# A transformer block with recurrent memory, forward and backward: products over a three-head block of tokens write 120 instead of 128 columns

## The chip, the cores and the metric

The kernel runs on one core of one Trainium2 chip. The metric is device microseconds per execution. A core has a TensorE (matrix products out of SBUF into PSUM), VectorE, ScalarE and GpSimd (in the profile PE, DVE, ACT and POOL; PEld is TensorE's loading of weights), and SyncE (SP), which here issues transfers. A matmul takes a stationary operand, loaded beforehand ("weights", lhsT), and streams a moving operand (rhs) past it: `out = lhsT.T @ rhs`. A turn (transpose) is a matmul whose moving operand is the identity.

## What is computed

Two blocks with an adaptive layer norm: an attention that carries eight memory tokens from segment to segment, and a gated feed-forward. The outputs are the block's result and the gradients of eleven inputs. Cut to the part around the change:

```python
for s in range(n_seg):                                   # 64 segments of 32 tokens
    h = jnp.concatenate([mem, x[:, s*32:(s+1)*32]], axis=1)   # 8 + 32 = 40 tokens
    q = jnp.einsum('btd,dhe->bhte', h, Wq)               # 32 heads of 128
    k = jnp.einsum('btd,dhe->bhte', h, Wk)
    v = jnp.einsum('btd,dhe->bhte', h, Wv)
    scores = jnp.einsum('bhqe,bhke->bhqk', q, k) * scale
    scores = jnp.where(mask[None, None], scores, -1e9)
    p = _softmax(scores, axis=-1)
    o = jnp.einsum('bhqk,bhke->bhqe', p, v)
    o = jnp.einsum('bhte,hed->btd', o, Wo)
    mem = o[:, :8]                                       # carried on
    outs.append(o[:, 8:])
...
_out, _vjp = jax.vjp(_f, ...)                            # and the gradients
```

Since the memory is carried, the 64 segments run one after another, forward in one direction and backward in the other.

## The kernel before

After a short setup, four stages follow each other on the core: the forward recurrence (`phase2`, roughly 30 to 1010 us), the feed-forward with its backward (`phase3`, to about 1525 us), the backward recurrence (`phase4`, to about 2510 us) and the gradients of the attention's weights (`phase5`, to the end).

**Tiling of the recurrences.** Three heads of 40 tokens are put side by side: 120 tokens. 32 heads make `G` = 11 such groups. Each group has a slot of `GW` = 128 columns in tiles of 11 x 128, so eight columns of each slot belong to no token. The groups are worked in `NP` = 3 parts of at most `PG` = 4 groups (4, 4 and 3); a part fills one PSUM bank. `part3(t, pi)` is a view of a part's slots in an SBUF tile.

**A forward round** (one segment). PE projects q, k and v, turns them, forms the scores (L724, whose moving operand has 120 columns), ACT takes the exponentials into ET, PE forms O (L759), DVE and ACT scale it into `Ost` (token rows, 120 of 128 filled, the rest zero). `ott(pi)` turns `Ost` by `transposes_part` (L737): four matmuls with the identity (L742) per part, and `evac` (L56; its copies show as L61 on ACT, L63 on DVE) copies the result to OT. The output projection (L223, `at_ps`) reads OT; OT and Ost are stored for the backward.

**A backward round** (one segment; loop from NS-1 to 0 in `phase4`). The order of every engine's instructions is the order of the code, fixed by `pin`. On PE, in this order:

- the projection of dy through Wo's transpose (L255) into RAd; `turn` (L1480): turns of RAd, which ACT and DVE copy into dOT (slots of 120 columns)
- dV' first part (`grad_mm("dVT", dOst, Pst, 0)`, L1614): weights dOst, moving Pst
- `dp` (L1593): weights dOT, moving VT, three parts; meanwhile DVE forms dO x O in place in OT (`prod`, L1578)
- dV' second part; `dost(2)`: turns of dOT (L1526); then `ds` (L1601): weights OT, moving a tile of -1, added onto dP in the same PSUM bank; DVE makes dS of it, times scale and Pst (L1603)
- dVT times Wv's transpose (L215), dV' third part, dV rows (`grad_mm("dV", Pst, dOst)`, weights Pst, moving dOst)
- `dstt`: turns of dS (L1526), copied to dST by ACT, DVE, ACT
- dK' (weights Qst, moving dS), copied to dKT by DVE; dQ' (`grad_mm("dQT", Kst, dST)`, weights Kst, moving dST), copied to dQT by ACT
- dKT, the rest of dVT and dQT times the weights' transposes (L215, L223), sums over the heads (L323), ACT's copy into the next round's dyT, and the next projection

In ACT's order stand, around the turns of dS: dVT part 2, dV rows part 0, dST part 0, dV rows part 2, dST part 2, then the three parts of dQT. In DVE's: dV rows part 1, dST part 1, the three parts of dKT.

SP loads OT, PS and VT (352 KB each) a round ahead into two buffers, and Qst and Kst (120 rows of the 128) into one buffer each; it also issues the DMA transposes of the whole dKT and dQT into rows, which POOL stores. POOL copies RAd into rows 0 to 95 of dOst; the rows of the tails come by three small DMAs of POOL (`dO_tails`, L1546).

Ahead of the loop, `ptiles` (L1425) makes the tiles and clears those with `zero=True` by a POOL memset (L1430): dS, dOst, then Qst and Kst. dST, dVT, dKT and dQT are not cleared. Behind the memsets POOL copies the first round's tails into dOT (L65) and issues dOst's first DMAs; SP's first loads of Qst and Kst wait for these tiles' memsets.

Of the kernel before, what the change touches and what calls it, by code (L numbers as in the profile page):

```python
# [40 lines left out]
class K:  # L41
# [395 lines left out]
    def phase2(self):  # L437
        nc, tc, cfg, io = self.nc, self.tc, self.cfg, self.io
        D, DC, H, E, L, M, T, G, NS = cfg.D, cfg.DC, cfg.H, cfg.E, cfg.L, cfg.M, cfg.T, cfg.G, cfg.NS
        GW = 128  # L440
        NP = 3
        PG = 4
# [8 lines left out]
        with ExitStack() as ctx:  # L451
# [13 lines left out]
            def ps_b16(name):  # L465
                return psp.tile([128, PG, GW], BF16, name=name, tag="p")

            def ptiles(name, n, zero=True, w=G * GW):
                ts = []
                for i in range(n):  # L470
                    t = pt.tile([128, w], BF16, name=f"{name}{i}")
                    if zero:
                        zeros.append(lambda t=t, w=w: nc.vector.memset(t[:, 1024:w] if w == 9 * 128 else t[:], 0.0))
                    ts.append(t)
                return ts
# [7 lines left out]
            Ost = ptiles("Ost", 1)[0]  # L483
            OT = ptiles("OT", 1)[0]
# [71 lines left out]
            def part3(t, pi):  # L556
                return t[:, pi * PW:min((pi + 1) * PW, G * GW)].rearrange("p (g x) -> p g x", x=GW)
# [131 lines left out]
            for s in range(NS):  # L689
# [44 lines left out]
                    a, b = a * PG, min(b * PG, G)  # L734
                    nc.vector.reciprocal(rden[:, a:b], ps[0:120, PG - 1, a:b])

                def transposes_part(src, pi, w=GW):  # L737
                    ps = ps_b16("tps")
                    n = min(PG, G - pi * PG)
                    for j in range(n):  # L740
                        g = pi * PG + j
                        nc.tensor.transpose(ps[:, j, :], src[:, g * w:g * w + GW], self.ident[:, :])  # L742
                    return ps[:, 0:n, :], n

                def vshift():
                    sh = ps_f32("sh_ps")
# [25 lines left out]
                                            rden[:, pi * PG:pi * PG + n].unsqueeze(2).to_broadcast([120, n, 128]), op=ALU.mult)  # L772

                def ott(pi):
                    ps, n = transposes_part(Ost, pi)
                    self.evac("dve" if pi == 1 else "act", part3(OT, pi)[:, 0:n, :], ps)

                def outproj():
                    ps = psp.tile([128, 256], F32, name="at_ps", tag="p")
# [57 lines left out]
                Pst = sb2.tile([128, G, 128], BF16, name="Pst", bufs=1)  # L837
# [29 lines left out]
                if more and not turned:  # L867
                    mask_mm(more.pop(0))
                    mask_mm(more.pop(0))
                ott(0)  # L870
                if len(more) > 1:
                    mask_mm(more.pop(0))
                ott(1)
                if len(more) > 1:
                    mask_mm(more.pop(0))
                ott(2)
                if more:
                    mask_mm(more.pop(0))
# [39 lines left out]
            for pi in range(NP):  # L918
                ps, n = transposes_part(ET, pi)
# [4 lines left out]
            for pi in range(NP):  # L924
                ps, n = transposes_part(Vst, pi)
# [472 lines left out]
    def phase4(self):  # L1398
        nc, tc, cfg, io = self.nc, self.tc, self.cfg, self.io
        D, DC, H, E, L, M, T, G, NS = cfg.D, cfg.DC, cfg.H, cfg.E, cfg.L, cfg.M, cfg.T, cfg.G, cfg.NS  # L1400
        GW = 128
# [4 lines left out]
        with self.p4_ctx as ctx:  # L1406
            WqT, WkT, WvT, WoT, negones = self.WqT, self.WkT, self.WvT, self.WoT, self.negones
# [8 lines left out]
            PG = 4  # L1416
            PW = PG * GW

            def ps_f32(name):
                return psp.tile([128, PG, GW], F32, name=name, tag="p")  # L1420

            def ps_b16(name):
                return psp.tile([128, PG, GW], BF16, name=name, tag="p")

            def ptiles(name, n, zero=True):  # L1425
                ts = []
                for i in range(n):
                    t = pt.tile([128, G * GW], BF16, name=f"{name}{i}")
                    if zero:
                        nc.gpsimd.memset(t[:], 0.0)  # L1430
                    ts.append(t)
                return ts

            dOT = pt.tile([128, cfg.XW], BF16, name="dOT")
# [4 lines left out]
            dSs = ptiles("dS", 1)  # L1439
            dSTs = ptiles("dST", 1, zero=False)  # L1440
            dOst_t = ptiles("dOst", 1)[0]
            dXTs = {nm: ptiles(nm, n, zero=False) for nm, n in (("dVT", 1), ("dKT", 1), ("dQT", 1))}

            def part3(t, pi):
                return t[:, pi * PW:min((pi + 1) * PW, G * GW)].rearrange("p (g x) -> p g x", x=GW)
# [72 lines left out]
                    loads[s] = d  # L1518
                return loads[s]

            def transposes_part(src, pi, w=GW):
                ps = ps_b16("tps")
                n = min(PG, G - pi * PG)
                for j in range(n):
                    g = pi * PG + j
                    nc.tensor.transpose(ps[:, j, :], src[:, g * w:g * w + GW], self.ident[:, :])  # L1526
                return ps[:, 0:n, :]

            def load_rows(t, dram, s):
                if s >= 0:  # L1530
# [29 lines left out]
            for s in reversed(range(NS)):  # L1560
# [11 lines left out]
                VT, OT, Pst, Kst, Qst = ld["VT"], ld["OT"], ld["Pst"], Kst_t, Qst_t  # L1572
                dS, dST, dOst = dSs[0], dSTs[0], dOst_t
                dVT, dKT, dQT = dXTs["dVT"][0], dXTs["dKT"][0], dXTs["dQT"][0]
# [13 lines left out]
                def dp(pi):  # L1588
                    ps = dps[pi] = ps_f32("dp_ps")
                    n = min(PG, G - pi * PG)  # L1590
                    for j in range(n):
                        g = pi * PG + j
                        nc.tensor.matmul(ps[:, j, :], lhsT=dOT[:, g * 120:g * 120 + GW], rhs=VT[:, g * GW:(g + 1) * GW],  # L1593
                                         start=(j == 0), stop=False, skip_group_check=True)

                def ds(pi):
                    ps = dps[pi]
                    n = min(PG, G - pi * PG)
                    for j in range(n):
                        g = pi * PG + j  # L1600
                        nc.tensor.matmul(ps[:, j, :], lhsT=OT[:, g * GW:(g + 1) * GW], rhs=negones[:, :],  # L1601
                                         start=False, stop=True, skip_group_check=True)
                    nc.vector.scalar_tensor_tensor(out=part3(dS, pi), in0=ps[:, 0:n, :], scalar=cfg.scale, in1=part3(Pst, pi),  # L1603
                                                   op0=ALU.mult, op1=ALU.mult)

                def grad_part(nm, lh, rh, xt, pi, eng):
                    grad_out(nm, xt, pi, eng, grad_mm(nm, lh, rh, pi))

                def grad_mm(nm, lh, rh, pi):
                    ps = ps_f32("g_ps")  # L1610
                    n = min(PG, G - pi * PG)
                    for j in range(n):
                        g = pi * PG + j
                        nc.tensor.matmul(ps[:, j, :], lhsT=lh[:, g * GW:(g + 1) * GW], rhs=rh[:, g * GW:(g + 1) * GW],  # L1614
                                         start=True, stop=True)
                    return ps

                def grad_out(nm, xt, pi, eng, ps):
                    self.evac(eng, part3(xt, pi), ps[:, 0:min(PG, G - pi * PG), :])
                    if pi == NP - 1 and nm != "dVT":  # L1620
                        rows = rxp.tile([128, G, 128], BF16, name="rows_x")
                        nc.sync.dma_start(rows[:], xt[:, :], transpose=True)
                        dram = {"dKT": self.DKR, "dQT": self.DQR}[nm][s]
                        row_stores.append(lambda: nc.gpsimd.dma_start(dram, rows[:]))
# [5 lines left out]
                    self.evac(eng, rv_rows[:, pi * PG:pi * PG + n, :], ps[:, 0:n, :])  # L1630

                def dstt(pi):
                    ps = transposes_part(dS, pi)
                    self.evac("dve" if pi == 1 else "act", part3(dST, pi), ps)

                dh_ps = [None]
                n_dh = [0]
# [27 lines left out]
                turn(0)  # L1665
                turn(1)
                gv0 = grad_mm("dVT", dOst, Pst, 0)
                prod(0)
                dp(0)
                prod(1)  # L1670
                dp(1)
                prod(2)
                dp(2)
                gv1 = grad_mm("dVT", dOst, Pst, 1)
                grad_out("dVT", dVT, 0, "act", gv0)
                if b_done:
                    b_done()
                dost(2)
                grad_out("dVT", dVT, 1, "act", gv1)
                ds(0)  # L1680
                ds(1)
                ds(2)
                self.pop_later()
                dht(dVT, WvT, 0)
# [17 lines left out]
                rv_out(0, "act", gr0)  # L1702
                rv_out(1, "dve", gr1)
                dstt(0)
                rv_out(2, "act", gr2)
                row_stores.append(lambda s=s, rows=rv_rows: nc.gpsimd.dma_start(self.DVR[s], rows[:]))
                dstt(1)
                dstt(2)
                gks = [grad_mm("dKT", Qst, dS, pi) for pi in range(NP)]
                load_rows(Qst_t, self.QST, s - 1)  # L1710
# [22 lines left out]
                g = s // 4  # L1733
# [428 lines left out]
```

## Time and profile before

| | us |
|---|---|
| three runs | 3092.86, 3091.20, 3092.27 |
| median | 3092.27 |
| the profiled execution: span from its first to its last instruction | 3090.4 |

The mean granted TensorE clock over the span is 0.991 of full speed. A "busy" matmul is one that has been issued and has not ended; matmuls overlap, so busy time is not the time that a matmul costs. In the lines of the prediction a row of the timeline is: start us, how long the row lasts us, engine, line, operation, out<-in, partitions x columns, and xN, the number of instructions merged in the row; in brackets, the idle time of the engine before it and what ended it. For a matmul the shape reads rows * columns of the weights, then partitions x columns of the result. The longest groups of the backward recurrence on PE, for a sense of proportion (lines of the page; count, busy us, mean ns):

| line, what | count | busy us | mean ns |
|---|---|---|---|
| L215 dh_ps<-WvT,dVT, 512 columns | 2048 | 133.6 | 381 |
| L223 dhq_ps<-WqT,dQT, 256 columns | 4096 | 122.9 | 273 |
| L215 dh_ps<-WkT,dKT, 512 columns | 2048 | 122.3 | 380 |
| L1614 g_ps<-Pst_l,dOst, 128 columns | 704 | 71.8 | 221 |
| L1593 dp_ps<-VT_l,dOT, 128 columns | 704 | 60.8 | 222 |
| L1614 g_ps<-dST,Kst, 128 columns | 704 | 59.5 | 218 |

### The profile page before, as it was taken

The numbers are of one execution on the slowest core, as the hardware profiler recorded it, in microseconds if no ns is written. First come the engines' busy times: TensorE is split into PE (matmuls) and PEld (weight loads), VectorE is DVE, ScalarE is ACT, GpSimd is POOL, SyncE is SP. The second block draws the span as 40 slices with busy tenths as digits, with TensorE's granted clock in tenths as the row PEclk, the third lists the DMA queues.
The fourth block names the chain that finished last, engine by engine and source line by source line (L and its number), as shares of the span: only waits on it lengthen the run. The fifth ranks groups of instructions, "written<-read, shape, count | busy, mean of one in ns | idle before, by whom it ended". The sixth has DMA issues, their size and how long they took to land.

```text
span 3090.4 us, 106123 instructions
## 1 busy us (share of the span) xinstructions
PE 3001.3 (97%) x43845; PEld 1831.6 (59%) x43845; DVE 1630.0 (53%) x3799; ACT 1268.9 (41%) x3056; POOL 1379.6 (45%) x2958
## 2 busy tenths in 40 slices
PE   6999999999998899989999999999999999999999
PEld 3666666666665444445577777777777754445455
DVE  4556656665555788732255555555555642322221
ACT  2555555555555433322255555555555530111011
POOL 3666766667766222211244444444444422333322
PEclk8999999999999999999999999999999999999999
DMA  8888788788778899997599999999999998666574
GB/s 299 215 216 202 203 211 215 205 211 216 200 201 261 201 232 230 226 280 246 169 237 245 246 244 242 241 248 242 247 240 246 243 277 282 197 197 220 191 238 147
DMA packets 845992, 703.54 MB, mean 228 GB/s; under 512 B 544354, under 2 KB 717954, under 8 KB 845124
## 3 DMA queue, kind: packets, MB, share of 16 engines
q1 hardware_dynamic: 714196, 486.69, 62.4%
q0 software_dynamic: 60656, 148.64, 15.1%
q10 hardware_dynamic: 70656, 61.41, 6.3%
q8 instruction: 345, 5.65, 0.8%
q14 instruction: 139, 1.14, 0.1%
HBM read 294.93 MB, written 276.35 MB: 185 GB/s over the span
## 4 chain that ended last, share of the span: by engine, by line
PE 86%; DMA 5%; issue 4%; DVE 2%; POOL 1%; SPq 1%; ACT 0%; POOLq 0%; DVEq 0%; ACTq 0%
PE pass_ps L255 18%; PE gps L1952 9%; PE dh_ps L215 8%; PE g_ps L1614 6%; PE gps5o L1966 4%; PE at_ps L223 4%; PE dhq_ps L223 4%; PE gps L1301 3%; PE mm L1145 3%; PE dh_tps L215 3%; PE turn_ps L264 2%; PE dp_ps L1593 2%; PE tps L1526 2%; PE tps L742 2%; PE mm L1105 2%
## 5 line engine op out<-in xcount | busy, mean ns | idle before, releaser
L1952 PE MATMUL gps<-rows,hrows 128*128 128x512 bf16 (+2 forms) x2160 | 417.5, 356 | 0.0
L1952 PEld LDWEIGHTS <-hrows 128*128 128x128 bf16 x2160 | 211.3, 98 | 204.5
L255 PEld LDWEIGHTS <-hT 128*32 128x32 bf16 x6144 | 158.6, 97 | 169.2 <-DMA Wq<-in_A_Wq_dram 6.0
L1658 POOL COPY dOst<-RAd 96x512 bf16<-96x512 bf16 x128 | 75.4, 612 | 312.7 <-DVE RAd L63 312.5
L63 DVE CAST ot<-gps 128x512 bf16<-128x512 f32 (+3 forms) x76 | 48.1, 634 | 288.3 <-PE gps L1952 198.4
L1956 POOL DMA_DIRECT2D out_dram<-ot x108 | 81.4, 753 | 255.4 <-DVE ot L63 140.2
L61 ACT ACTIVATE ot<-gps 128x512 bf16<-128x512 f32 (+3 forms) x75 | 41.3, 551 | 355.1 <-PE gps L1952 216.1
L909 POOL TENSOR_TENSOR Pst<-Pst,rden 120x1408 bf16<-120x1408 bf16 x63 | 159.7, 2534 | 49.4 <-issue 21.8
L61 ACT ACTIVATE dVT<-g_ps 128x512 bf16<-128x512 f32 (+1 forms) x192 | 109.5, 570 | 96.3 <-PE g_ps L1614 95.6
L63 DVE CAST RA0v<-pass_ps 128x512 bf16<-128x512 f32 x128 | 88.6, 692 | 90.4 <-PE pass_ps L255 86.8
L255 PE MATMUL pass_ps<-Wv,hT 128*32 128x512 bf16 x2048 | 134.2, 382 | 0.0
L215 PE MATMUL dh_ps<-WvT,dVT 128*32 128x512 bf16 x2048 | 133.6, 381 | 0.2 <-DVE RBd L63 0.2
L1966 PE MATMUL gps5o<-WoT,rows 128*128 128x512 bf16 x592 | 128.5, 379 | 1.4 <-DMA rows<-OSR 1.4
L255 PE MATMUL pass_ps<-Wq,hT 128*32 128x512 bf16 x2048 | 123.3, 383 | 5.8 <-DMA Wq<-in_A_Wq_dram 5.8
L223 PE MATMUL at_ps<-Wo,OT 128*32 128x256 bf16 x4096 | 124.9, 275 | 3.8 <-DMA Wo<-in_A_Wo_dram 3.6
L255 PE MATMUL pass_ps<-Wk,hT 128*32 128x512 bf16 x2048 | 121.8, 380 | 2.2 <-ACT hT L899 1.1
L1603 DVE SCALAR_TENSOR_TENSOR dS<-dp_ps,Pst_l 128x512 bf16<-128x512 f32 (+1 forms) x192 | 112.1, 640 | 22.1 <-PE dp_ps L1601 22.1
L255 PE MATMUL pass_ps<-WoT,dyT 128*32 128x256 bf16 (+1 forms) x3072 | 122.5, 308 | 0.9 <-ACT dyT L1732 0.9
L223 PE MATMUL dhq_ps<-WqT,dQT 128*32 128x256 bf16 x4096 | 122.9, 273 | 0.0
L215 PE MATMUL dh_ps<-WkT,dKT 128*32 128x512 bf16 x2048 | 122.3, 380 | 0.0
L223 PEld LDWEIGHTS <-dQT 128*32 128x32 bf16 x4096 | 109.6, 97 | 15.8
L223 PEld LDWEIGHTS <-OT 128*32 128x32 bf16 x4096 | 103.9, 97 | 19.7 <-ACT OT L61 8.4
(419 smaller groups left out, 7073.6 us busy)
## 6 DMA issues: line engine op xcount, KB each, us to landing
OSR<-Ost SPq DMA_DIRECT2D x64, 352.0 KB
OT<-OT SPq DMA_DIRECT2D x64, 352.0 KB
VT<-VTr SPq DMA_DIRECT2D x64, 352.0 KB
PS<-Pst SPq DMA_DIRECT2D x64, 352.0 KB
OT_l<-OT SPq DMA_DIRECT2D x64, 352.0 KB
Pst_l<-PS SPq DMA_DIRECT2D x64, 352.0 KB
VT_l<-VT SPq DMA_DIRECT2D x64, 352.0 KB
DVR<-rows_x POOLq DMA_DIRECT2D x64, 352.0 KB, 6.2
```

The costliest lines, as they stand in the source:

```text
L61: return nc.scalar.activation(out, in_, AF.Copy)
L63: return nc.vector.tensor_copy(out, in_)
L215: self.nc.tensor.matmul(ps[32 * j:32 * j + 32, :], lhsT=lhsT, rhs=w, start=(n < 4), stop=(n >= total - 4), tile_position=(0, 32 * j))
L223: nc.tensor.matmul(ps[32 * j:32 * j + 32, :], lhsT=x[k], rhs=w[k][:, 256 * d:256 * d + 256], start=(n == 0), stop=(n == total - 1), tile_p ...
L255: self.nc.tensor.matmul(ps[32 * j:32 * j + 32, :], lhsT=lhs(c), rhs=rhs, start=(c == 0), stop=(c == DC - 1), tile_position=(0, 32 * j))
L909: nc.gpsimd.tensor_tensor(Pst[0:120, :, :], Pst[0:120, :, :], rden[:, :].unsqueeze(2).to_broadcast([120, G, 128]), op=ALU.mult)
L1145: nc.tensor.matmul(hp[:], lhsT=xT[:, fc, :], rhs=wT[:, fc, :], start=(n == 0), stop=(n == 2 * FC - 1))
L1301: nc.tensor.matmul(ps[:], lhsT=h2r[:, j, c * 128:(c + 1) * 128], rhs=xr[:, j, :], start=(j == 0), stop=(j == NT - 1))
L1603: nc.vector.scalar_tensor_tensor(out=part3(dS, pi), in0=ps[:, 0:n, :], scalar=cfg.scale, in1=part3(Pst, pi), op0=ALU.mult, op1=ALU.mult)
L1614: nc.tensor.matmul(ps[:, j, :], lhsT=lh[:, g * GW:(g + 1) * GW], rhs=rh[:, g * GW:(g + 1) * GW], start=True, stop=True)
L1952: nc.tensor.matmul(ps[:, 0:ng * E], lhsT=hrows[:, tp_, c * 128:(c + 1) * 128], rhs=rows[:, tp_, 0:ng * E], start=(tp_ == 0), stop=(tp_ == ...
L1966: nc.tensor.matmul(pss[gg][:], lhsT=src[0][:, src[1], gg * E:(gg + 1) * E], rhs=dyrows[:, tp_, :], start=(tp_ == order[0]), stop=(tp_ == o ...
```

## The change

Line numbers of the profile hold for the code before.

```diff
 # forward and backward alike
-def transposes_part(src, pi, w=GW):
+def transposes_part(src, pi, w=GW, m=128):
...
-        nc.tensor.transpose(ps[:, j, :], src[:, g * w:g * w + GW], self.ident[:, :])
-    return ps[:, 0:n, :]
+        nc.tensor.transpose(ps[:, j, 0:m], src[0:m, g * w:g * w + GW], self.ident[0:m, 0:m])
+    return ps[:, 0:n, 0:m]

 # forward
 def ott(pi):
-    ps, n = transposes_part(Ost, pi)
-    self.evac("dve" if pi == 1 else "act", part3(OT, pi)[:, 0:n, :], ps)
+    ps, n = transposes_part(Ost, pi, m=120)
+    self.evac("dve" if pi == 1 else "act", part3(OT, pi)[:, 0:n, 0:120], ps)

 # backward
-dXTs = {nm: ptiles(nm, n, zero=False) for nm, n in (("dVT", 1), ("dKT", 1), ("dQT", 1))}
+dXTs = {nm: ptiles(nm, n, zero=nm != "dVT") for nm, n in (("dVT", 1), ("dKT", 1), ("dQT", 1))}
...
 # dp
-nc.tensor.matmul(ps[:, j, :], lhsT=dOT[:, g * 120:g * 120 + GW], rhs=VT[:, g * GW:(g + 1) * GW],
+nc.tensor.matmul(ps[:, j, 0:120], lhsT=dOT[:, g * 120:g * 120 + GW], rhs=VT[:, g * GW:g * GW + 120],
                  start=(j == 0), stop=False, skip_group_check=True)
 # ds
-nc.tensor.matmul(ps[:, j, :], lhsT=OT[:, g * GW:(g + 1) * GW], rhs=negones[:, :],
+nc.tensor.matmul(ps[:, j, 0:120], lhsT=OT[:, g * GW:(g + 1) * GW], rhs=negones[:, 0:120],
                  start=False, stop=True, skip_group_check=True)
-nc.vector.scalar_tensor_tensor(out=part3(dS, pi), in0=ps[:, 0:n, :], scalar=cfg.scale, in1=part3(Pst, pi),
+nc.vector.scalar_tensor_tensor(out=part3(dS, pi)[:, :, 0:120], in0=ps[:, 0:n, 0:120],
+                               scalar=cfg.scale, in1=part3(Pst, pi)[:, :, 0:120],
                                op0=ALU.mult, op1=ALU.mult)
 # grad_mm
-nc.tensor.matmul(ps[:, j, :], lhsT=lh[:, g * GW:(g + 1) * GW], rhs=rh[:, g * GW:(g + 1) * GW],
+w = GW if nm == "dV" else 120
+nc.tensor.matmul(ps[:, j, 0:w], lhsT=lh[:, g * GW:(g + 1) * GW], rhs=rh[:, g * GW:g * GW + w],
                  start=True, stop=True)
 # grad_out
-self.evac(eng, part3(xt, pi), ps[:, 0:min(PG, G - pi * PG), :])
+self.evac(eng, part3(xt, pi)[:, :, 0:120], ps[:, 0:min(PG, G - pi * PG), 0:120])
 # dstt
-ps = transposes_part(dS, pi)
-self.evac("dve" if pi == 1 else "act", part3(dST, pi), ps)
+ps = transposes_part(dS, pi, m=120)
+self.evac("dve" if pi == 1 else "act", part3(dST, pi)[:, :, 0:120], ps)
```

The stationary operands keep their 128 columns; the moving ones, and with them the results, have 120. The two kinds of turns also load 120 instead of 128 rows of weights. The copies behind these products read and write 120 of each slot's 128 columns. dKT and dQT, which DMA transposes read whole, are cleared once before the loop; in POOL's order these two memsets stand behind dOst's and ahead of those of Qst and Kst, and in SP's order the first loads of Qst and Kst now stand behind the second round's loads of Pst and VT. Otherwise each engine has the same instructions in the same order. dV's rows and the turns of dOT (`dost`) are left as they were.

More of the change, by code (lines that the diff above doesn't have):

```diff
@@ L741, in transposes_part @@
                         g = pi * PG + j
-                        nc.tensor.transpose(ps[:, j, :], src[:, g * w:g * w + GW], self.ident[:, :])
-                    return ps[:, 0:n, :], n
+                        nc.tensor.transpose(ps[:, j, 0:m], src[0:m, g * w:g * w + GW], self.ident[0:m, 0:m])
+                    return ps[:, 0:n, 0:m], n
                 def vshift():
@@ L1519, in get_loads, with transposes_part @@
                 return loads[s]
-            def transposes_part(src, pi, w=GW):
+            def transposes_part(src, pi, w=GW, m=128):
                 ps = ps_b16("tps")
@@ L1525, in transposes_part @@
                     g = pi * PG + j
-                    nc.tensor.transpose(ps[:, j, :], src[:, g * w:g * w + GW], self.ident[:, :])
-                return ps[:, 0:n, :]
+                    nc.tensor.transpose(ps[:, j, 0:m], src[0:m, g * w:g * w + GW], self.ident[0:m, 0:m])
+                return ps[:, 0:n, 0:m]
             def load_rows(t, dram, s):
```

## The prediction

> **What bounds the kernel now.** I read the page first, then the windows by stage, then one round of the backward loop instruction by instruction. The page:
>
> ```profile
> span 3090.4 us, 106123 instructions
> PE 3001.3 (97%) x43845; PEld 1831.6 (59%) x43845; DVE 1630.0 (53%) x3799; ACT 1268.9 (41%) x3056; POOL 1379.6 (45%) x2958
> PE 86%; DMA 5%; issue 4%; DVE 2%; POOL 1%; SPq 1%; ACT 0%; POOLq 0%; DVEq 0%; ACTq 0%
> ```
>
> TensorE is busy 97% of the span and carries 86% of the chain that ended last. The two recurrences, forward and backward, in windows (columns: length, busy time of PE, PEld, DVE, ACT, POOL, granted clock, DMA share, GB/s):
>
> ```profile
> 60.00:1010.00 950.00, 929.39 (x17421) 581.14 (x17413) 561.52 (x1420) 500.19 (x1330) 647.74 (x1383) 1.00 0.81 213
> 1540.00:2510.00 970.00, 967.18 (x19963) 693.60 (x19965) 571.88 (x1403) 521.57 (x1314) 442.47 (x1101) 1.00 0.97 243
> ```
>
> In the backward one PE is idle for 3 us of 970, at the full granted clock. But "busy" counts each matmul's latency (219 ns for 128 columns), and they overlap; what a matmul costs is the distance from its start to the next start. A row of n back-to-back matmuls of latency d that lasts t gives (t-d)/(n-1):
>
> ```profile
> 512.00 0.61 PE L264 MATMUL turn_ps<-ident,RA1q 128*128 128x128 bf16 x8
> 513.52 0.59 PE L724 MATMUL st_ps<-qT,kT 128*128 128x120 bf16 x8
> 1499.75 2.24 PE L1301 MATMUL gps<-Wv,Wk 128*128 128x448 bf16 x11
> ```
>
> 128 columns: (0.61-0.219)/7 = 56 ns. 448 columns, latency 0.352: 2.24-0.352 over 10 = 189 ns. The slope is (189-56)/320 = 0.415 ns a column, so eight columns are worth 3.3 ns. The forward scores (L724) already write 120 columns into slots of 128, as the changed products will: (0.59-0.216)/7 = 53 ns, which agrees. So the saving per matmul is real and small.
>
> One backward round (15.12 us; loads of weights where they waited, and ACT's own row of work):
>
> ```profile
> 1814.44 0.39 PE L1614 MATMUL g_ps<-Pst_l,dOst 128*128 128x128 bf16 x4
> 1814.69 0.96 PE L1593 MATMUL dp_ps<-VT_l,dOT 128*128 128x128 bf16 x11
> 1815.03 0.45 PEld L1593 LDWEIGHTS <-dOT 128*128 128x128 bf16 x8 [0.17 <-ACT dOT L61]
> 1815.88 0.78 PE L1601 MATMUL dp_ps<-negones,OT_l 128*128 128x128 bf16 x11
> ...
> 1818.05 0.34 PE L1614 MATMUL g_ps<-Pst_l,dOst 128*128 128x128 bf16 x3
> 1818.43 0.49 ACT L61 ACTIVATE dVT<-g_ps 128x384 bf16<-128x384 f32 x1 [1.37 <-PE g_ps L1614]
> 1818.82 0.59 ACT L61 ACTIVATE rows_x<-g_ps 128x512 bf16<-128x512 f32 x1
> 1819.30 0.60 ACT L61 ACTIVATE dST<-tps 128x512 bf16<-128x512 bf16 x1
> 1819.46 0.82 PE L1614 MATMUL g_ps<-dS,Qst 128*128 128x128 bf16 x11
> 1819.77 0.51 ACT L61 ACTIVATE rows_x<-g_ps 128x384 bf16<-128x384 f32 x1
> 1820.12 0.93 PE L1614 MATMUL g_ps<-dST,Kst 128*128 128x128 bf16 x11
> 1820.14 0.53 ACT L61 ACTIVATE dST<-tps 128x384 bf16<-128x384 bf16 x1
> ```
>
> Eleven unhindered matmuls take 0.78 (L1601). dP takes 0.96: after three of its eleven it waits for ACT's copy into dOT. dK takes 0.82 and dQ 0.93: 0.04 and 0.15 are waits. dQ's last three cannot start before ACT has copied the third part of dS' transpose, which ends at 1820.14+0.53 = 1820.67; counted back from dQ's end (1821.05 - 0.219 - 2 x 0.056) they start at 1820.72. ACT works without a pause from 1818.43, released by the last dV' product (1818.05+0.34 = 1818.39). So between that product and dQ's last three, ACT's five copies set the time, not PE.
>
> **The change part by part.** Per backward round 66 matmuls lose eight columns: 11 each of dV', dP, dS' row sums, turns of dS, dK', dQ'. At 3.3 ns that is 220 ns; what is kept of it:
> - dV's first four and dP's first three: they run into the wait for dOT, which hangs on the unchanged turns of dO. Hidden: 0 of 23 ns. Without that wait they would pay all 23.
> - dP's last eight, dV's next four, the row sums' eleven, dV's last three: 26 x 3.3 = 86 ns, all on the chain. Behind them stands nothing late: ACT's second dVT copy ends at 1817.06 and its users start near 1817.3, and the copy moves up with them.
> - turns, dK' and dQ's first eight (30 x 3.3 = 99 ns): hidden behind ACT's five copies. There counts what ACT saves. ACT's copy takes 597 ns at 512 and 490 at 384 elements, 0.84 ns an element; the forward's exponentials write the same gapped 4 x 120 shape and take 568, where the slope gives 570, so gaps cost nothing. Three of the five copies shrink (24, 32, 24 elements): 20+27+20 = 67 ns. The waits for dK and dQ grow instead by 99-67 = 32 ns.
> - dQ's last three: 10 ns.
>
> Sum 86+67+10 = 163 ns a round, times 64 = 10.4 us. If ACT's copies gained nothing, 6.1; if every wait vanished with it, 14.1.
>
> VectorE's side (dS, dK' and one dS' copy): 692 ns at 512, 558 at 384 (L771), 1.05 ns an element, so 34 and 25 ns less each. dK's second part is copied at 1821.31 and its matmuls come 12 x 54 ns after 1820.97, at 1821.62: 0.3 us spare, and both move up by about 80. The dS' copy takes 425 ns for 512 bf16; copies in gapped patterns take 348 for 384 (kT), so no loss of speed there. Priced at nothing; with that cover gone the 34 ns of a copy is the most that is won.
>
> Forward: eleven turns of O per round, 11 x 3.3 = 36 ns, on the chain before the output projection; three rounds of four show them unhindered, in the fourth they wait for O itself (11 in 857 ns instead of 615) and keep about a third. 64 x (0.75 x 36 + 0.25 x 12) = 1.9 us. Bounds 0 and 2.3.
>
> Weights of 120 rows (both kinds of turns) appear nowhere at this size. Loads with 128 columns and few rows do: 4 rows took 100 ns, 8 rows 91, against 98 for 128 rows. I take no cost. The far end is the mask's 120 x 120 load, 172 ns (once, at 5.5 us, and with fewer columns).
>
> Start of the backward: POOL clears two more tiles ahead of Qst and Kst, and SP's loads of Qst and Kst move behind the second round's Pst_l and VT_l.
>
> ```profile
> 1528.34 1.27 POOL L1430 MEMSET Qst<- 128x1408 bf16 x1
> 1531.48 1.54 POOL L1546 DMA_DIRECT2D dOst<-RBd  x3
> 1538.33 0.59 PE L1614 MATMUL g_ps<-Pst_l,dOst 128*128 128x128 bf16 x4 [6.37 <-DMA dOst<-RBd]
> ```
>
> A clear takes 1.21 us start to start, so dOst's transfer is issued 2.4 us later, and PE waits for just that transfer. If its flight stays as it was, the loss is 2.4 us. But it took 5-6 us behind eight big loads, against a median of 4.7 to landing; two of these loads, which SP held from 1527.7 to 1531.2 behind Qst and Kst, now leave earlier and are out of its way. POOL's own copies into dOst (1533.50+1.30) would end at 1537.2, 1.1 us before PE starts now: the best case. Between -1.1 and +2.4 I take 0. Qst and Kst, first read at 1545.05 and 1545.70, would be issued near 1532 and 1533: covered by 12 us.
>
> Total 10.4+1.9 = 12.3 us off the profiled 3090.4: 3078.1. That execution lies 1.9 us under the median of 3092.27, so the forecast is **3080 us**.
>
> The Trainium skill's "TensorE: Matmul & The Clock Gate", in "Back-to-back issue gap", speaks against the change: in a stream of weight load and matmul pairs it gives about 81 ns per pair at 128 columns, the load taking its share, so that fewer columns would bring PE nothing. The traced 56 and 53 ns contradict it; by it the sum would fall to ACT's share. "PSUM — Partial Sum Buffer" (Specifications) says that non-contiguous patterns slow matmuls; L724, in gapped slots, shows no such thing.
>
> **The rivals.**
> - The backward is held by transfers. For: DMA share 0.97 there. Then only the forward's 1.9 remains: 3090. Against: no wait of PE for a DMA between 1600 and 2400; the tails of dOst are issued at 1820.25, land after 4.7 and are needed at 1829.55; one round with fewer matmuls took 14.6 us (1569.6 to 1584.2) at share 0.95 with the same loads. 9%.
> - The copies set more than I see: only ACT's 67 ns count, 64 x 67 = 4.3 us: 3088. Against: the 86 ns stretch shows no wait after dP's. 8%.
> - Every saved column counts, because the copies move up too: 14.1+2.3: 3076. 9%.
> - Slower: weight loads of 120 rows are as slow as the mask's. Place: 22 turns a round, 1408 in all; price 172-98 = 74 ns each, 104 us: about 3184. It decides from 12.3/1408 = 9 ns a turn on. Against: the 4- and 8-row loads. 4%.
>
> **How the numbers follow.** The forecast has 70%, with its own range 3078 to 3085 (ACT's gain none, the start at +2.4 or -1.1). For 8 in 10 I reach over the full gain and up to the second rival: 3075 to 3088. A measurement here tells 0.2% (6.2 us) from nothing. Faster: forecast and full gain, and a little of the second rival, 81%; same: transfers and the rest of the second, 15%; slower 4%.
>
> **What would show it.** Right: 11 row sums in 0.74 us, a backward round near 14.96 instead of 15.12, dP still waiting for dOT, dQ's wait grown a little, first dV' near 1538. Wrong: turns of dS above 56 ns apiece, waits of PE for Qst, Kst or VT_l, dS' copies on ACT not shorter than 600 ns.

## The result and the profile after

| | us |
|---|---|
| before, median of 6 runs (3090.93 to 3093.93) | 3092.43 |
| changed, median of 6 runs (3080.64 to 3084.83) | 3081.94 |
| ratio, 95% interval | 0.9968 (0.9956 to 0.9979) |
| profiled span, before and changed | 3090.4 and 3078.9 |

The change takes 10.5 us off the median and 11.5 us off the profiled span; the forecast was 12.3 off the span (3078.1) and 3080 for the time. A second set on another chip gave 3093.65 and 3083.51 us, a ratio of 0.9969 (0.9957 to 0.9980).

The first lines are from the page of the changed kernel.

```profile
span 3078.9 us, 106050 instructions
PE 2985.9 (97%) x43769; PEld 1821.5 (59%) x43845; DVE 1613.0 (52%) x3799; ACT 1254.4 (41%) x3056; POOL 1386.1 (45%) x2960
```

PE is as full as before, 97%. The two recurrences in the windows used before:

```profile
60.00:1010.00 950.00, 927.17 (x17433) 579.50 (x17425) 561.07 (x1423) 497.85 (x1330) 649.27 (x1383) 1.00 0.81 213
1540.00:2510.00 970.00, 965.14 (x20163) 688.94 (x20160) 559.98 (x1412) 511.01 (x1317) 444.18 (x1100) 1.00 0.99 246
```

The full clock was granted again, and the DMA share rose from 0.97 to 0.99: the same bytes in less time. Busy time says nothing of the gain here. What does is the length of a round, from the first turn of RAd (L1480) to the next round's. There are four kinds of round, by what else stands in them (projections and tails of four segments), and most rounds of a kind (9 to 14 of some 16) agree with their median within 3 ns, in the profiles from every chip used; in one kind each of three profiles only 7 or 8 do. That makes 10 ns a round visible where the times of one kernel on one chip scatter by 3 to 9 us. In all that follows a kind is given by its median over 15 or 16 rounds:

| kind | before, ns | changed, ns | difference |
|---|---|---|---|
| 1 | 15112 | 14950 | -162 |
| 2 | 15088 | 14925 | -163 |
| 3 | 15287 | 15123 | -164 |
| 4 | 15745 | 15642 | -103 |

The forecast was 163 in every round. Three kinds give it to within a nanosecond; the fourth gives 60 less. From the first round's turn to the last round's the backward took 970.83 us before and 961.12 after, 9.7 less (forecast 10.4). The table makes 9.3 of it; the rest lies in single rounds, above all the first and the fourth, which were 0.48 and 0.46 us shorter. The forward rounds lost 22.7 ns each, 1.4 us in all (forecast 1.9). What is left of the 11.5 us, 0.4, is the scatter of the stages that the edit does not touch.

One round of the changed kernel in the timeline, most of the rows that were shown of before, and the turns of dS:

```profile
1810.02 0.93 PE L1593 MATMUL dp_ps<-VT_l,dOT 128*128 128x120 bf16 x11
...
1810.36 0.43 PEld L1593 LDWEIGHTS <-dOT 128*128 128x128 bf16 x8 [0.17 <-ACT dOT L61]
...
1811.17 0.74 PE L1601 MATMUL dp_ps<-negones,OT_l 128*128 128x120 bf16 x11
...
1813.67 0.47 ACT L61 ACTIVATE dVT<-g_ps 128x360 bf16<-128x360 f32 x1 [1.35 <-PE g_ps L1616]
...
1814.09 0.74 PE L1526 MATMUL tps<-ident,dS 120*128 120x120 bf16 x11
...
1814.52 0.58 ACT L61 ACTIVATE dST<-tps 128x480 bf16<-128x480 bf16 x1
1814.68 0.78 PE L1616 MATMUL g_ps<-dS,Qst 128*128 128x120 bf16 x11
...
1815.30 0.91 PE L1616 MATMUL g_ps<-dST,Kst 128*128 128x120 bf16 x11
1815.34 0.50 ACT L61 ACTIVATE dST<-tps 128x360 bf16<-128x360 bf16 x1
```

The row sums take 0.74 us, as predicted. dP still waits 0.17 us for ACT's copy into dOT. ACT's three copies shrank from 0.49, 0.60 and 0.53 to 0.47, 0.58 and 0.50. dK' and dQ' in all eleven products went from 0.82 and 0.93 to 0.78 and 0.91: both still wait, since eleven unhindered ones take 0.74. What dQ' waits for can be read off: its ninth product starts 50 ns after ACT's third copy of dS' ends, before and after alike, and 0.21 us after its eighth. Summed from start to start, the groups of a round of the first kind, in ns:

| PE group | before | changed | difference |
|---|---|---|---|
| dP, 11 | 795 | 768 | -27 |
| dV' next 4 | 224 | 210 | -14 |
| row sums, 11 | 614 | 578 | -36 |
| dV' last 3 | 178 | 168 | -10 |
| turns of dS, 11 | 615 | 596 | -19 |
| dK', 11 | 655 | 617 | -38 |
| dQ', 11 | 859 | 840 | -19 |

The first four rows make 87 (forecast 86, "all on the chain"), the last three 76 (forecast 67+10 = 77). A row runs to the start of the next group, so a wait ahead of that counts with it: the turns themselves lost 31 ns from the first start to the last, and 12 of them went into a longer wait of dK's first product, which starts 50 ns after ACT's copy of dV's first rows ends.

Now the fourth kind. Around dVT's first product with WvT, first before, then changed (timeline):

```profile
1861.39 0.69 DVE L63 CAST RBd<-pass_ps 128x512 bf16<-128x512 f32 x1
...
1861.97 0.22 PE L335 MATMUL dh_b_tp<-ident,dh_b_tb 128*128 128x128 bf16 x1
...
1862.13 0.83 PE L215 MATMUL dh_ps<-WvT,dVT 128*32 128x512 bf16 x12
```

```profile
1856.23 0.68 DVE L63 CAST RBd<-pass_ps 128x512 bf16<-128x512 f32 x1
...
1856.74 0.22 PE L335 MATMUL dh_b_tp<-ident,dh_b_tb 128*128 128x128 bf16 x1
...
1856.97 0.81 PE L215 MATMUL dh_ps<-WvT,dVT 128*32 128x512 bf16 x9
```

`pass_ps` of `proj_b`, which projects the tails of four segments into RBd, and `dh_ps` use one PSUM bank (tag "dh"), so dVT's product cannot start before DVE has copied `pass_ps` out. That copy stands behind DVE's products (L1578), which hang on dOT, and so it did not move with PE: it ends at 1862.08 before and 1856.91 after, and counted from the first turn of the round that is 2.61 us both times. The single turn moved up from 2.51 to 2.43 us of its round; the product stayed at 2.66, some 50 ns behind the copy's end. Before, the gap from the single turn to the product was 0.16 us, afterwards 0.23: here some 76 ns that PE had just won were waited away.

### The profile page after: what moved, and what is told of

It reads as the page before. It is cut to its first block, busy times and chain, and to the rows that moved or that the text cites. A ratio compares the mean times of both kernels' runs of the same rounds, so it can differ in the third digit from the quotient of the medians.

```text
span 3078.9 us, 106050 instructions
## 1 busy us (share of the span) xinstructions
PE 2985.9 (97%) x43769; PEld 1821.5 (59%) x43845; DVE 1613.0 (52%) x3799; ACT 1254.4 (41%) x3056; POOL 1386.1 (45%) x2960
## 4 chain that ended last, share of the span: by engine, by line
PE 45%; issue 3%; POOL 1%; DMA 1%; DVE 0%; ACT 0%; SPq 0%; POOLq 0%
PE gps L1954 9%; PE dh_ps L215 8%; PE g_ps L1616 6%; PE pass_ps L255 5%; PE gps5o L1968 5%; PE dhq_ps L223 4%; PE dh_tps L215 3%; PE dp_ps L1593 2%; PE tps L1526 2%; PE dp_ps L1601 1%; PE turn_ps L1480 1%; PE dh_ft L323 1%; POOL out_dram L1958 1%; DMA dhb<-DHA 0%; PE turn_ps L264 0%
## 5 line engine op out<-in xcount | busy, mean ns | idle before, releaser
L61 ACT ACTIVATE dVT<-g_ps 128x480 bf16<-128x480 f32 (+1 forms) x192 | 104.7, 545 | 95.5 <-PE g_ps L1616 95.1
L215 PE MATMUL dh_ps<-WvT,dVT 128*32 128x512 bf16 x2048 | 133.4, 380 | 0.3 <-DVE RBd L63 0.2
L215 PE MATMUL dh_ps<-WkT,dKT 128*32 128x512 bf16 x2048 | 122.3, 380 | 0.0
L1603 DVE SCALAR_TENSOR_TENSOR dS<-dp_ps,Pst_l 128x480 bf16<-128x480 f32 (+1 forms) x192 | 106.1, 608 | 19.2 <-PE dp_ps L1601 19.2
```

What stands on the lines that cost most here:

```text
L61: return nc.scalar.activation(out, in_, AF.Copy)
L215: self.nc.tensor.matmul(ps[32 * j:32 * j + 32, :], lhsT=lhsT, rhs=w, start=(n < 4), stop=(n >= total - 4), tile_position=(0, 32 * j))
L1603: nc.vector.scalar_tensor_tensor(out=part3(dS, pi)[:, :, 0:120], in0=ps[:, 0:n, 0:120], scalar=cfg.scale, in1=part3(Pst, pi)[:, :, 0:120], ...
```

## Experiments

All lengths are medians by kind, in the order of the table above. Spans of single profiles are given only where they say something: the rounds are the finer measure.

**1. The copies without the products.** The kernel before, all matmuls at 128 columns, only the copies narrower (and dKT, dQT cleared as in the change, dST too):

```diff
-self.evac(eng, part3(xt, pi), ps[:, 0:min(PG, G - pi * PG), :])
+self.evac(eng, part3(xt, pi)[:, :, 0:120], ps[:, 0:min(PG, G - pi * PG), 0:120])
-self.evac("dve" if pi == 1 else "act", part3(dST, pi), ps)
+self.evac("dve" if pi == 1 else "act", part3(dST, pi)[:, :, 0:120], ps[:, :, 0:120])
 # dS' scalar_tensor_tensor: 120 columns of each slot, as in the change
```

> The kernel before, with every product and turn 128 columns wide as it was; only the copies out of them (ACT's for dV' and dS', DVE's for dS, dK' and one dS') and ACT's for dQ' take 120 of each 128 columns. Theory: from dV's last product to dQ's last three it is ACT's five copies that set the time, and three of them shrink by 24, 32 and 24 elements at 0.84 ns: 20+27+20 = 67 ns in each of the 64 backward rounds. The four kinds of round (15112, 15088, 15287, 15745 ns before) each become 67 ns shorter, dQ's last three start that much earlier, the span falls by 4.3 us. First rival, PE's columns alone count: rounds unchanged within 10 ns. Second rival, the copies do all that the change does: 163 ns a round.

Measured: 15046, 15022, 15220 and 15681 ns: 66, 66, 67 and 64 less than before. In the timeline the copies shrank and the products did not:

```profile
1818.58 0.47 ACT L61 ACTIVATE dVT<-g_ps 128x360 bf16<-128x360 f32 x1 [1.40 <-PE g_ps L1616]
...
1819.61 0.78 PE L1616 MATMUL g_ps<-dS,Qst 128*128 128x128 bf16 x11
...
1820.23 0.91 PE L1616 MATMUL g_ps<-dST,Kst 128*128 128x128 bf16 x11
1820.26 0.49 ACT L61 ACTIVATE dST<-tps 128x360 bf16<-128x360 bf16 x1
```

dK' and dQ' at 128 columns take the 0.78 and 0.91 us that they take in the changed kernel at 120: it is ACT's copies that set both. The edit narrows DVE's copies too; that the 66 ns are ACT's is read from the trace, in which dQ's ninth product again starts 52 ns after ACT's third copy ends. The backward as a whole lost 3.7 us (967.16 against 970.83); the span only 0.4, because this execution reached the backward 1.8 us later and took 1.5 us more behind it.

**2. The hidden products wide again.** The changed kernel, 37 of its 66 products and turns back at 128 columns (and dST cleared ahead of the loop):

```diff
 # dp
+w = GW if g < 3 else 120
 # grad_mm
-w = GW if nm == "dV" else 120
+w = GW if nm in ("dV", "dKT") or (nm, pi) in (("dVT", 0), ("dQT", 0), ("dQT", 1)) else 120
 # dstt
-ps = transposes_part(dS, pi, m=120)
+ps = transposes_part(dS, pi)[:, :, 0:120]
```

> The changed kernel, with 37 of the 66 products and turns of a backward round back at 128 columns: dV's first four, dP's first three, the eleven turns of dS, dK's eleven and dQ's first eight; the copies stay at 120. Theory: all of them run into a wait that they do not set (dP's for the copy into dOT, dQ's last three for ACT's third copy of dS'), so the 37 x 3.3 = 122 ns are taken out of these waits (now 170, and 46+20+156 = 222 ns) and the rounds stay at 14950, 14925, 15123 and 15642 ns, within 10. First rival, every column pays: 122 ns a round, 7.8 us. Second rival, loads of 120 rows cost something in the turns: the eleven turns of dS, back at 128 rows, take less than the 595 ns that they take now, instead of 615.

Measured: 14950, 14925, 15123 and 15661 ns. Three kinds did not move by even a nanosecond; the fourth grew by 19. The loop as a whole took 962.64 us, 1.5 more than the changed kernel's; the kinds explain 0.3 of that, and the rest stands in single rounds, the longest of them 0.64 us over its kind, which no run took apart. The timeline shows why nothing is lost in the others:

```profile
1810.06 0.93 PE L1595 MATMUL dp_ps<-VT_l,dOT 128*128 128x128 bf16 x11
...
1814.13 0.78 PE L1527 MATMUL tps<-ident,dS 128*128 128x128 bf16 x11
...
1814.74 0.78 PE L1618 MATMUL g_ps<-dS,Qst 128*128 128x128 bf16 x11
...
1815.36 0.90 PE L1618 MATMUL g_ps<-dST,Kst 128*128 128x128 bf16 x11
```

dP's row is as long as in the changed kernel, 0.93. The turns grew from 0.74 to 0.78, and dK' and dQ' swallowed it: the stretch from the first turn to the end of dQ' is 2053 ns there and 2054 here (first kind, start to start). So in three kinds of four more than half of the edited products and turns bring nothing in this kernel. The turns with 120 rows of weights and 120 columns start 53 ns apart, those with 128 and 128 here 56: loads of 120 rows cost nothing, and the slower rival is out. In the fourth kind a single turn stands between dK' and dQ', so the waits lie differently there, and 19 ns were left over.

**3. The copy that holds the bank.** The changed kernel, RBd's second half copied by ACT:

```diff
-return lambda: self.evac(("act", "dve")[hf], RBds[t % 2][:, 512 * hf:512 * hf + 512], ps[:])
+return lambda: self.evac("act", RBds[t % 2][:, 512 * hf:512 * hf + 512], ps[:])
```

> The changed kernel, with one copy moved: RBd's second half is copied out of pass_ps by ACT and no longer by DVE. Theory: in every fourth round dVT's first product with WvT waits for that bank, whose copy stands behind DVE's products and did not move with the change; there 76 ns of the saving were lost. On ACT the copy fits between dOT and dOst (0.48 us idle before dOst) and ends near 1856.5 on the scale where it now ends at 1856.91; the fourth kind of round falls from 15642 to about 15566 ns, the others stay, the span falls by 1.2 us. Rival: the copy pushes ACT's second dVT copy past its users, and the fourth kind grows by up to 100 ns.

Measured: 14949, 14925, 15123 and 15566 ns; the fourth kind lost exactly the 76. (The loop as a whole lost only 0.6 us of the 1.2: three of the first eight rounds were 0.2 to 0.4 us longer than in the changed kernel.)

```profile
1854.26 0.65 ACT L61 ACTIVATE RBd<-pass_ps 128x512 bf16<-128x512 f32 x1
...
1855.27 0.22 PE L335 MATMUL dh_b_tp<-ident,dh_b_tb 128*128 128x128 bf16 x1
...
1855.42 1.26 PE L215 MATMUL dh_ps<-WvT,dVT 128*32 128x512 bf16 x18
```

The copy ends half a microsecond before the bank is wanted, and the gap from the single turn to the product is 0.15 us again.

**4. The same on the kernel before** (the same edit).

> The kernel before, with the copy of RBd's second half moved from DVE to ACT. Theory: in the fourth kind of round the bank was already late before the change (free at 1862.08, dVT's first product with WvT at 1862.13), so this round gets shorter here too, by 10 to 25 ns: with the copy on ACT in both kernels the change is worth 163 ns in the fourth kind as in the others (15566 + 163 = 15729 here, instead of 15745). Rival: the fourth kind loses its 60 ns elsewhere, and stays at 15745 here, so that the change is worth 179 there with the copy moved in both; or it falls by more than 40, and the bank held this kernel more than it holds the changed one.

Measured: 15113, 15089, 15287 and 15741 ns. The fourth kind won 4, not 10 to 25: before the change the bank came free just in time. With the copy on ACT in both kernels the change is worth 15741-15566 = 175 ns there, more than the 163 expected. The group sums put some 12 of it into the copies' stretch: dQ' lost 43 ns instead of 20, the single turn ahead of it gained 10. The rival's 179 is thus nearer in size, but its ground, a loss elsewhere, is not: the loss was at the bank.

**5. One of ACT's copies to DVE.** The changed kernel:

```diff
 # dstt
-self.evac("dve" if pi == 1 else "act", part3(dST, pi)[:, :, 0:120], ps)
+self.evac("dve" if pi else "act", part3(dST, pi)[:, :, 0:120], ps)
```

> The changed kernel, with one copy moved: the third part of dS' turn is copied by DVE and no longer by ACT. Theory: ACT's copies set the time up to dQ's last three. With the last of them on DVE (0.31 us for 360 bf16 elements, ending near 1815.44 instead of 1815.84) the waits in dK and dQ (46+20+156 = 222 ns) go, but DVE's first dK' copy ends 0.3 us later, near 1816.04, and dK's first product with WkT, which could start at 1815.95, waits for it: 100 to 150 ns a round are won, 6 to 10 us. First rival, free banks and not dS' set it: dQ's last three wait for a bank all the same, below 30 ns a round. Second rival: DVE's later dK' copies hold the products with WkT, and the round grows by up to 100 ns.

Measured: 14806, 14780, 14981 and 15539 ns: 144, 145, 142 and 103 less. The loop took 952.1 us instead of 961.1. (Its one time, 3067.74 us beside 3093.26 for the kernel before, gains besides from an early start of the backward, at 1524.9 us.)

```profile
1821.78 0.65 DVE L63 COPY dST<-tps 128x480 bf16<-128x480 bf16 x2
...
1822.35 1.21 DVE L63 CAST dKT<-g_ps 128x480 bf16<-128x480 f32 x2
1822.35 0.76 PE L1616 MATMUL g_ps<-dST,Kst 128*128 128x120 bf16 x11
...
1823.05 0.62 PE L215 MATMUL dh_ps<-WkT,dKT 128*32 128x512 bf16 x8
```

dQ' now runs in 0.76 us instead of 0.91: its last three products no longer wait. The start of dKT's products at 1823.05 lies 0.70 after dQ's start; it was 0.84 in the changed kernel. So the wait that the prediction read off the timeline ("ACT's five copies set the time, not PE") was real, and one word in the code removes most of it. Smaller waits stay: some 18 ns at dK's first product and 20 at dQ's fifth, which start about 50 ns after ACT's two copies of dV's rows end, and 46 at dK's third part, whose first product starts 50 ns after ACT's first copy of dS' ends. And now DVE ends the stretch, as the expectation said: it copies without a pause from dV's rows over dS' second and third part to dK's first, and dKT's first product starts 54 ns after that last copy ends (337 in the changed kernel).

**6. The hidden products wide, with that copy on DVE** (edits 2 and 5 together).

> The kernel with 37 products and turns back at 128 columns (dV's first four, dP's first three, dS' turns, dK, dQ's first eight), now with dS' third copy on DVE. Theory: with ACT's last copy out of the way little of the wait is left in the stretch (46 ns at dK's third part, 20 in dQ), so the columns hidden before now cost part of their 99 ns: 20 to 55 ns a round over 14806, 14780, 14981 and 15539; dV's and dP's stay hidden. First rival: still hidden, below 10 ns. Second rival: every column pays, 122 ns.

Measured: 14822, 14799, 14997 and 15550 ns: 16, 19, 16 and 11 over experiment 5. Less than expected. The trace shows by what way the 16 come: the first eight turns end 25 ns later, DVE's copy of dS' second part now has to wait for them and ends 16 later, and with it all of DVE's copies up to dK's first, behind which dKT's first product again starts after 55 ns. The wider columns of dK' and dQ' still cost nothing, now under DVE's copies in place of ACT's.

**7. The forward taken back.** The changed kernel with O's turns and their copies at 128 columns.

> The changed kernel with the forward's part taken back: O's eleven turns and the copies out of them are 128 columns wide again. Theory: the forward gained by this alone, 22.7 ns a round (14745.3 to 14722.6 ns, mean of 60 rounds), so its rounds go back to 14745 and the span grows by 1.4 us; the backward rounds stay at 14950, 14925, 15123 and 15642 ns. Rival: the forward's difference came from elsewhere (the state of the chip), and its rounds stay at 14723.

Measured: the forward rounds (two by two, from one turn of RA1q to the next; mean of 29) take 29488 ns, against 29442 in the changed kernel and 29487 before: 23 ns a round, as expected. Backward rounds: 14949, 14925, 15123, 15642. The span grew by 6.9 us, of which the rounds explain 1.5; the backward was entered at 1535.4 instead of 1529.6 us. Entries into the backward lay between 1524.9 and 1535.4 us over all the profiles, which bounds what one span can prove.

**8. A kernel with the waits taken away, at both widths.** Edits 3 and 5, and dV's second four products moved into dP's wait:

```diff
-dp(0)
+dp(0, 0, 3)                                   # products 0 to 2
+gv1 = grad_mm("dVT", dOst, Pst, 1)
+dp(0, 3)                                      # product 3
 prod(1)
...
 dp(2)
-gv1 = grad_mm("dVT", dOst, Pst, 1)
```

On the kernel before:

> The kernel before (all widths 128) with three steps that take waits away: RBd's second half is copied by ACT, dS' third part by DVE, and dV's second four products stand between dP's third and fourth, where PE waited for the copy into dOT. Theory: dP's wait (about 170 ns) is filled by the four products, and dQ's wait shrinks: 250 to 330 ns a round less than before, the kinds near 14810, 14790, 14990 and 15430, the span 16 to 21 us shorter. Rival: the row sums, which then come 0.17 us earlier, wait for DVE's products instead, and only the 100 to 150 ns at dQ are won.

On the changed kernel:

> The same three steps on the changed kernel. Theory: 144 ns (dQ) + 150 to 174 ns (dP) less than the changed kernel in each round, and 76 more in the fourth kind: near 14640, 14615, 14815 and 15260; the time near 3060. With the waits gone, more of the narrower columns count: against the same steps at 128 columns the change is worth 180 to 220 ns in every kind instead of 163, 163, 164 and 103. Rival: the change stays at 163 a round, since PE is then held by other copies.

Measured: 14801, 14775, 14976 and 15462 ns at 128 columns (0.9952 of the kernel before, 0.9939 to 0.9966), and 14640, 14616, 14817 and 15293 at 120 (0.9917, 0.9904 to 0.9931; 3068.9 us). dP's wait is filled, in the timeline of the second:

```profile
1675.19 0.33 PE L1595 MATMUL dp_ps<-VT_l,dOT 128*128 128x120 bf16 x3
...
1675.36 0.38 PE L1618 MATMUL g_ps<-Pst_l,dOst 128*128 128x120 bf16 x4
...
1675.58 0.59 PE L1595 MATMUL dp_ps<-VT_l,dOT 128*128 128x120 bf16 x8
```

The rounds came out as computed, but for 33 ns in the fourth kind. The time did not: 3068.9 us, where 3060 was expected (the kernel before took 3096.03 on this chip). And the change is worth 161, 159, 159 and 169 ns here, not 180 to 220. From group to group, dP and dV's second four give 34 instead of 41, the last stretch 80 instead of 76, and there it is DVE's copies that count: at both widths dKT's first product starts 55 ns after DVE's first dK' copy ends. Counted from the first product of dV's rows, that end comes 79 ns earlier at 120 columns, since these copies are shorter (dS' second part 396 instead of 425 ns, dK's first 646 instead of 680). The rival was right: with ACT's last copy out of the way PE is held by other copies, and in place of the wider range nearly the same 163 came out.

**9. All on one chip: the changed kernel, the two moved copies, and the version of 8.**

> The changed kernel itself, on the same chip as the next three: 0.9968 of the kernel before, rounds of 14950, 14925, 15123 and 15642 ns.

> The changed kernel with two copies moved: RBd's second half to ACT, dS' third part to DVE. Theory: the two gains add, 144 ns in each round and 76 more in the fourth kind: 14806, 14780, 14981 and 15463 to 15470 ns, 11 us less than the changed kernel. Rival: the fourth kind keeps its 15539, since ACT then delays dVT's second copy.

> The two copies moved and dV's second four products between dP's third and fourth, again, beside the kernel with the two copies alone. Theory: 166 ns a round less than that one, 10.6 us. Rival: the shorter rounds bring nothing more in time, because PE then stops for issue gaps of 0.1 to 2 us in single rounds (as one round of 17298 ns in the earlier profile), with the transfers at a share of 1.02: less than 5 us between the two.

| | time, us | ratio to before | kinds, ns |
|---|---|---|---|
| changed | 3083.51 | 0.9969 (0.9957 to 0.9980) | 14949, 14925, 15123, 15642 |
| two copies moved | 3075.17 | 0.9939 (0.9926 to 0.9951) | 14804, 14776, 14980, 15457 |
| and dV' into dP's wait | 3069.34 | 0.9921 (0.9908 to 0.9935) | 14641, 14615, 14816, 15293 |

The two gains add, as expected (the fourth kind even 15457). The last step gives its 161 to 164 ns in each kind, but 5.8 us in the median where 64 rounds make 10.4. In the profiles the whole loop is 3.7 us shorter (947.1 against 950.8), and part of the difference is seen: the first round is 1.2 us longer than with the two copies alone, the next three 0.17 to 0.18 each, and one round is 2.7 us longer than others of its kind. So the theory's 10.6 us did not come; whether it was more than the rival's 5, medians of five and of four runs, each over a range of 3 to 5 us, do not tell.

## Why the forecast held, and where it did not

- **Price of a column.** "3.3 ns per matmul": eleven row sums lost 36 ns, 3.3 each. Right, and in gapped slots too.
- **On the chain, 86 ns.** Measured 87 in three kinds of four.
- **Hidden, and ACT's saving in its place, 67 ns.** Experiment 1 isolates 66; experiment 2 shows 0 for the hidden 37. These two together show that the 163 split as was said. The second rival (only copies count) is out by the other 97, the third (every column counts) by experiment 2. The waits that take up the hidden columns are of two sorts that the prediction did not tell apart: dQ's last three wait for dS' itself, dK' and dQ's fifth for a bank that one of ACT's copies frees (read from the traces).
- **"Behind them stands nothing late."** This failed in the fourth kind. It was read from one round, in which DVE makes no copy of RBd. In every fourth round that copy holds the bank for dVT's product, and 76 ns of waiting stand there (experiment 3), 4 of them from before (experiment 4). Less the 12 ns that the last stretch gives more in this kind, it is 60 short: over some 15 rounds 0.9 us. The term was 10.4; 9.7 was measured, and that it came so near is in part luck, the 0.4 us of single rounds.
- **Forward, 1.9 us.** The turns do save 36 ns in two of the three kinds of round where O is not late (233 to 220, and the like, per part of four) and 24 in the third, and 10 where O is late. But in two of these kinds the mask's products behind the turns (L667), up to the next group, take 14 and 25 ns more than they did, so the four kinds kept 12, 14, 22 and 42 ns. A quarter of the term was lost. That the mask's products then wait for something that did not move is inferred from this alone, and no run took it apart.
- **Start of the backward, 0.** From the first turn of RAd to the first dV' it took 7.21 us before and 7.46 after. The other two profiles without the two clears gave 7.14 and 7.53, those with them 7.00 to 7.64 and once 8.51. No cost stands out of the scatter.
- **Transfers as the bound.** Rounds shrank at a share of 0.99, and by 144 ns more in experiment 5 with a share of 1.00 (1530 to 2480 us): out for this change.
- **Loads of 120 rows.** Out: the turns start 53 ns apart with them and 56 with 128 rows.
- **Two readings beside the sum.** "So that fewer columns would bring PE nothing" is the prediction's own reading of the 81 ns, which the page does not say; the row sums lost 3.3 ns each. And the scores (L724) cannot speak on non-contiguous patterns: each product writes 120 adjoining columns, and the gaps lie between the products.

## What to carry to other kernels

A saving on the busiest engine counts only up to the next thing that does not move with it; so go through the stretch and ask, for each wait, which of its suppliers moves up too, and do it for every kind of iteration, not for one. Moving a copy to another engine moves the wait with it: after experiment 5 it is DVE's copies that hold PE. Where an engine that is 97% busy still waits, its last supplier may be one small copy: moving one 0.5 us copy to another engine gave nearly as much as narrowing 66 products a round. And where the iterations repeat to a few nanoseconds, compare their lengths: they settle in one execution differences far below the 3 to 9 us by which the total scatters.

## What was not expected

In the two profiles of the version of 8 on the changed kernel PE stopped once for about 2 us in the middle of dVT's products, with no wait of its own that the profile shows. The row after the gap, in the first of them:

```profile
1679.77 0.61 PE L215 MATMUL dh_ps<-WvT,dVT 128*32 128x512 bf16 x7 [1.62 <-issue]
```

"issue" marks idle time that nothing shown ended. In the loop PE's loading of weights for these products (L215) lost 2.7 and 4.4 us to it in the two profiles, against 0.2 with the two copies alone; the DMA share between 1540 and 2470 us was 1.02 in both, and 0.99 there. The same version at 128 columns, at a share of 1.00, stopped once for 1.0 us at another line (L323). Whether the transfers starve the stream of instructions was not tried; it stays open, as does the rest of the 10.4 us that the shorter rounds did not bring.
